# Batch 0's head: q by head halves, narrow weight slices and a reordered chain

## The chip, the cores and the metric

One NeuronCore of a Trainium2 chip runs the whole kernel. The metric is the device time of one execution in microseconds (us); lower is better. "Span" is the time from the first to the last instruction that the profile shows; the device time is 1.7 to 2.0 us longer in all executions of the kernel before that are listed with their spans. Two times within 2% of each other are called the same.

## The reference, cut to what matters

```python
def _attn_ref(q, k, v, g_norm):                    # q, k, v: 8 batches x 8 heads x 576 x 64
    kv = np.einsum('bhsd,bhse->bhde', k, v)        # K^T V, 64 x 64 per head
    out = np.einsum('bhsd,bhde->bhse', q, kv)      # scores
    rms = np.sqrt(np.mean(out * out, axis=-1, keepdims=True) + 1e-06)
    return out / rms * g_norm

def reference(...):
    x = attn_out.transpose(0, 2, 1, 3).reshape(4608, 512)
    h = x @ w_in                                   # w_in: 512 x 2048
    g = np.where(h > 0.0, h, np.exp(np.minimum(h, 0.0)) - 1.0)
    return g @ w_out                               # w_out: 2048 x 512
```

## The kernel before

Eight batches of 512 rows and a ninth group made of the leftover rows go through attention, a first layer and a second layer. From some 20 us on, TensorE works nearly without pause. Only batch 0's beginning is special: its x is made transposed, in four column parts c (two heads each), because nothing else can keep TensorE busy yet. The helpers of that head:

```python
    def kv_first(c):                       # K^T V of the heads of part c, cast to bf16 on VectorE
        u, l = c // 2, c % 2
        kv_single(0, kv_ps, u, (l,))
        ls = slice(l * 64, l * 64 + 64)
        nc.vector.tensor_copy(out=kv0[ls, u], in_=kv_ps[ls, :, u * 64 : u * 64 + 64])

    def se_first(c):                       # scores of part c: needs q of pairs u and 2 + u
        u, l = c // 2, c % 2
        ls = slice(l * 64, l * 64 + 64)
        for s in range(2):
            nc.tensor.matmul(se0[c][s * 64 : s * 64 + 64, :], lhsT=kv0[ls, u, s, :],
                             rhs=qT0[ls, 2 * s + u, :], start=True, stop=True)

    def square_first(c):  nc.scalar.activation(sq0[c], se0[c], AF.Square)
    def mean_first(c):    nc.tensor.matmul(mean0[c], lhsT=means, rhs=sq0[c], start=True, stop=True)
    def log_first(c):     nc.scalar.activation(r0[c], mean0[c], AF.Ln, bias=eps_col)
    def exp_first(c):     nc.scalar.activation(r0[c], r0[c], AF.Exp, scale=-0.5)
    def scale_first(c):   nc.vector.scalar_tensor_tensor(out=x0[:, c, :], in0=se0[c], scalar=g_col,
                                                         in1=r0[c], op0=ALU.mult, op1=ALU.mult)
    def first(fs, cs):                     # products of w_in's column blocks f with x's parts c
        for c in cs:
            for f in fs:
                nc.tensor.matmul(products[f], lhsT=w_in_sb[:, c, f * P : f * P + P], rhs=x0[:, c, :],
                                 start=(c == 0), stop=(c == KC - 1))
    def idle(ps, n):                       # dummy products on zeros, to keep TensorE's clock up
        for _ in range(n):
            nc.tensor.matmul(ps, lhsT=zeros[:, 0:P], rhs=zeros, start=True, stop=True)
```

(Formatting of the one-line helpers is condensed here.) The loads and the order of the head before the change:

```python
    fetch_q(0)                             # two 512 KB loads on SyncE's queue: even heads, then odd heads
    ...                                    # k and v in four parts each on GpSimd's queue, cast to bf16 on the way
    edges = (0, 512, 768, 1280, 1664, 2048)
    for lo, hi in zip(edges, edges[1:]):
        load_w_in(slice(lo, hi))           # 512 rows x (hi - lo) columns, also on GpSimd's queue, cast to bf16
    ...
    idle(idle_ps, 9)
    ...                                    # cast and transpose q of pairs 0, 1; idle(idle_ps, 4); then q of pair 2
    kv_first(0); idle(idle_ps, 1); se_first(0); square_first(0)
    ...                                    # transpose q of pair 3
    kv_first(1); mean_first(0); log_first(0); se_first(1); square_first(1); exp_first(0)
    ...                                    # g_col, one tiny product
    kv_first(2); idle(idle_ps, 2); se_first(2); square_first(2)
    mean_first(1); log_first(1); exp_first(1)
    idle(idle_ps, 1); kv_first(3); scale_first(0); idle(idle_ps, 1)
    mean_first(2); log_first(2); se_first(3); square_first(3); exp_first(2)
    idle(bank(0), 2); scale_first(1); scale_first(2)
    first((0, 1, 2, 3), (0,))
    mean_first(3); log_first(3); exp_first(3); scale_first(3)
    first((0, 1, 2, 3), (1, 2)); first((4,), (0, 1, 2)); first((0, 1, 2, 3), (3,))
    first((5,), (0, 1, 2)); first((4, 5), (3,))
    ...
    for i in range(3, 8):
        mm1(0, i, ...)()                   # from here on: the regular stream of TensorE
```

Later, batch 1's attention is woven into batch 0's second layer (`mm2`); its second K^T V (`at["kvu1"]()`) came after step j == 1 of one of those loops.

## Time and profile before

| | kernel before |
|---|---|
| time, median of 3 | 284.08 us (284.08 to 284.27) |
| the profiled execution | 284.47 us, span 282.7 us |
| first v part landed | 7.81 us |
| first scores | 8.96 us |
| first product with w_in | 14.76 us |
| last part of x scaled | 17.43 to 18.18 us |
| regular stream starts | 20.27 us |

In the timeline, each line gives start, microseconds taken, engine, source line, operation, what it writes and reads, the shape, and how many instructions were joined; brackets at the end give how long the engine had been idle and who ended that. PEld is the load of weights into TensorE. "L465" is the first layer's product in the kernel before. The lines that the prediction quotes stand there; three more of the kernel before matter, from the timeline of the head (K^T V of part 0; the products with the last scaled part; the start of the stream):

```profile
8.11 0.47 PE L174 MATMUL kv_ps<-v_pk,k_pk 64*64 64x64 bf16 x18
...
18.33 0.59 PE L674 MATMUL h_ps<-xT,w_in_sb 128*128 128x512 bf16 x2
...
20.27 0.59 PE L465 MATMUL h_ps<-xT,w_in_sb 128*128 128x512 bf16 x2
```

The first is the start of K^T V, which needs v (landed at 7.81): it began 0.3 us after that.

### The profile page before, as it was taken

How to read it: one execution, taken by the hardware profiler on the slowest of the kernel's cores; microseconds unless marked ns; L12 is line 12 of the kernel's file. 1: busy time of each engine (PE TensorE's matmuls, PEld its weight loads, DVE VectorE, ACT ScalarE, POOL GpSimd, SP SyncE). 2: the span in 40 equal slices, each digit the busy share in tenths (PEclk: the TensorE clock that was granted, in tenths of full speed). 3: DMA queues.
4: the chain of work that ended last, by engine and by line, in shares of the span. 5: the costliest groups of instructions: out<-in, count | busy, mean ns of one | idle time of the engine just before them, and what ended most of it. 6: DMA issues, size and time to landing. Idle time of an engine off the chain costs nothing.

```text
span 282.7 us, 5187 instructions
## 1 busy us (share of the span) xinstructions
PE 277.2 (98%) x2146; PEld 129.7 (46%) x2146; DVE 159.3 (56%) x231; ACT 154.5 (55%) x222; POOL 54.7 (19%) x96
## 2 busy tenths in 40 slices
PE   7999999999999999999999999999999999999994
PEld 3444454445444444444444444444444444444443
DVE  2359443878388646944694468445854585444400
ACT  2779546667487438533863377237923792333311
POOL 7834422261421331005200421012000000000000
PEclk9999999999999999999999999999999999999999
DMA  7999999797993696358935794455233122010122
GB/s 194 203 204 202 208 200 185 220 152 129 187 190 62 154 166 148 74 148 124 196 75 145 93 216 84 116 115 150 55 97 73 78 53 95 0 77 0 74 74 77
DMA packets 56523, 35.99 MB, mean 127 GB/s; under 512 B 32820, under 2 KB 54068, under 8 KB 56500
## 3 DMA queue, kind: packets, MB, share of 16 engines
q0 software_dynamic: 20752, 17.30, 39.9%
q1 hardware_dynamic: 35348, 17.83, 23.7%
q10 hardware_dynamic: 400, 0.52, 0.6%
q8 instruction: 17, 0.28, 0.4%
q14 instruction: 6, 0.05, 0.0%
HBM read 36.70 MB, written 9.44 MB: 163 GB/s over the span
## 4 chain that ended last, share of the span: by engine, by line
PE 95%; DMA 2%; DVE 1%; SPq 0%; issue 0%; ACT 0%
PE h_ps L465 41%; PE o_ps L512 39%; PE o_ps L917 5%; DMA st_q<-in_q_dram 2%; PE at L174 2%; PE bank L674 1%; PE at L465 1%; PE at L201 1%; PE h_ps L674 1%; PE bank L596 1%; PE bank L644 1%; PE se_ps L201 1%; PE kv_ps L174 0%; PE at L185 0%; PE se_ps L413 0%; PE bank L656 0%
## 5 line engine op out<-in xcount | busy, mean ns | idle before, releaser
L465 PE MATMUL h_ps<-xT,w_in_sb 128*128 128x512 bf16 x536 | 125.7, 379 | 0.0
L512 PE MATMUL o_ps<-w_out_sb,gT 128*128 128x512 bf16 x512 | 120.5, 379 | 0.0
L477 ACT ACTIVATE elu_e<-h_ps 128x1024 bf16<-128x1024 f32 (+1 forms) x71 | 70.0, 995 | 79.9 <-PE h_ps L465 78.3
L465 PEld LDWEIGHTS <-w_in_sb 128*128 128x128 bf16 x552 | 52.5, 98 | 63.2 <-DVE xT L333 1.7
L512 PEld LDWEIGHTS <-gT 128*128 128x128 bf16 x512 | 49.4, 98 | 58.4
L488 DVE TENSOR_SCALAR elu_e<-elu_e 128x1024 bf16<-128x1024 bf16 (+1 forms) x75 | 32.3, 431 | 72.9 <-ACT elu_e L477 72.9
L496 DVE TENSOR_TENSOR gT<-elu_e,h_ps 128x1024 bf16<-128x1024 bf16 (+1 forms) x51 | 60.1, 1179 | 5.7 <-DVE elu_e L488 0.5
L525 ACT COPY o_sb<-o_ps 128x512 f32<-128x512 f32 x32 | 18.6, 586 | 15.6 <-PE o_ps L512 15.6
L218 DVE TENSOR_REDUCE ss<-sq 128x16 f32<-128x1024 bf16 x16 | 19.4, 1219 | 10.8 <-ACT sq L213 10.1
L483 ACT ACTIVATE elu_h<-h_ps 128x1024 bf16<-128x1024 f32 (+1 forms) x20 | 19.5, 990 | 0.0
L150 POOL COPY q_bf<-q_pk 128x512 bf16<-128x512 bf16 x24 | 14.6, 638 | 21.6 <-DMA q_pk<-in_q_dram 21.6
L496 DVE TENSOR_TENSOR gT<-elu_e,elu_h 128x1024 bf16<-128x1024 bf16 x20 | 13.8, 692 | 2.9 <-ACT elu_h L483 1.5
L917 PE MATMUL o_ps<-w_out_sb,gT 128*128 128x512 bf16 (+1 forms) x80 | 14.1, 337 | 0.0
L125 POOL COPY gate<-qT 1x1 bf16<-1x1 bf16 x6 | 1.1, 182 | 63.7 <-DMA qT<-q_bf 63.7
L104 POOL DMA_DIRECT2D q_pk<-in_q_dram x14 | 10.6, 762 | 2.8 <-issue 1.1
L229 DVE TENSOR_TENSOR xs<-at,ss 128x512 bf16<-128x512 f32 x16 | 10.3, 682 | 1.2 <-ACT ss L225 1.2
L917 PEld LDWEIGHTS <-gT 128*128 128x128 bf16 x80 | 7.7, 98 | 6.4 <-DVE gT L496 0.4
L213 ACT ACTIVATE sq<-at 128x1024 bf16<-128x1024 f32 x9 | 9.4, 1043 | 1.6 <-PE at L201 1.0
L118 POOL DMA_DIRECT2D k_pk<-in_k_dram x12 | 8.3, 691 | 4.5 <-DMA w_in_sb<-in_moe_w_in_dram 2.9
L596 PE MATMUL bank<-zeros 128*128 128x512 bf16 x20 | 7.8, 515 | 1.2 <-DVE zeros L573 1.2
L118 POOL DMA_DIRECT2D v_pk<-in_v_dram x12 | 8.2, 684 | 3.7 <-DMA w_out_sb<-in_moe_w_out_dram 1.8
L925 ACT COPY o_last<-o_ps 128x512 f32<-128x512 f32 (+1 forms) x5 | 2.5, 501 | 10.8 <-PE o_ps L917 10.8
(79 smaller groups left out, 139.4 us busy)
## 6 DMA issues: line engine op xcount, KB each, us to landing
out_dram<-o_sb SPq DMA_DIRECT2D x16, 512.0 KB, 3.0
q_pk<-in_q_dram POOLq DMA_DIRECT2D x14, 256.0 KB, 4.8
k_pk<-in_k_dram POOLq DMA_DIRECT2D x6, 576.0 KB, 8.3
v_pk<-in_v_dram POOLq DMA_DIRECT2D x6, 576.0 KB, 10.8
st_q<-in_q_dram SPq DMA_DIRECT2D x2, 512.0 KB, 5.1
w_in_sb<-in_moe_w_in_dram POOLq DMA_DIRECT2D x2, 512.0 KB, 8.8
w_out_sb<-in_moe_w_out_dram POOLq DMA_DIRECT2D x2, 512.0 KB, 15.2
w_out_sb<-in_moe_w_out_dram POOLq DMA_DIRECT2D x4, 256.0 KB, 11.8
```

What stands on the lines that cost most here:

```text
L118: nc.gpsimd.dma_start(out=raw[name, b].rearrange("p h j d -> p h (j d)")[:, hs], in_=in_[:, hs])
L150: eng.tensor_copy(out=out_, in_=in_)
L218: nc.vector.reduce_sum(out=ss, in_=sq.rearrange("p c (h e) -> p (c h) e", h=H), axis=AX.X)
L465: nc.tensor.matmul(h_ps[a][:, cs], lhsT=w_in_sb[:, c, f * P : f * P + P], rhs=x(c, cs), start=(c == 0), stop=(c == KC - 1),)
L477: nc.scalar.activation(e[:, lo:hi, :], ps, AF.Exp)
L483: nc.scalar.activation(h[:, lo:hi, :], ps, AF.Relu)
L488: nc.vector.tensor_scalar(out=e[:, lo:hi, :], in0=e[:, lo:hi, :], scalar1=1.0, scalar2=1.0, op0=ALU.min, op1=ALU.subtract,)
L496: nc.vector.tensor_tensor(out=gT[T][:, 2 * i + lo : 2 * i + hi, :], in0=e[:, lo:hi, :], in1=h, op=ALU.add if relu else ALU.max,)
L512: nc.tensor.matmul(o_ps[T, j], lhsT=gT[T][:, f, j * P : j * P + P], rhs=w_out_sb[:, f, :], start=(f == 0), stop=(f == FC - 1),)
L525: nc.scalar.copy(o_sb[T][:, j % 2, :], o_ps.pop((T, j)))
L596: nc.tensor.matmul(ps, lhsT=zeros[:, 0:P], rhs=zeros, start=True, stop=True)
L917: nc.tensor.matmul(ps, lhsT=gT[B][:, f, j * P : j * P + P], rhs=w_out_sb[:, f, cols], start=(f == 0), stop=(f == FC - 1),)
```

## The change

The intent is to start the regular stream earlier by closing the waits of the head: feed the first scores from the first half of q, keep ScalarE's chain (square, logarithm, exponential) dense, get the first weights sooner in narrower slices, and do the products slice by slice. The core of the diff, with cuts marked:

```diff
-    fetch_q(0)
-    q_raw0 = raw.pop(("q", 0))
+    q_raw0 = stage_tile("q")[:, 0:2048].rearrange("p (u x) -> p u x", u=2)
+    for u in range(2):
+        nc.sync.dma_start(
+            out=q_raw0[:, u].rearrange("p (h x) -> p h x", h=4),
+            in_=q[0, 4 * u : 4 * u + 4, 0:G, :].rearrange("h (p j) d -> p h (j d)", j=J),
+        )
...
-    edges = (0, 512, 768, 1280, 1664, 2048)
+    edges = (0, 256, 512, 768, 1024, 1280, 1664, 2048)
...
-    cast_first(1, A)
+    cast_first(2, A)
...            # pairs 0 and 2 are cast and turned first, then 1 and 3
+    g_ps = bank(2)                                   # g_col's product, moved up from behind exp_first(0)
+    nc.tensor.matmul(g_ps[:, 0:1], lhsT=..., rhs=one, start=True, stop=True)
+    nc.vector.tensor_copy(out=g_col, in_=g_ps[:, 0:1])
     kv_first(0)
-    idle(idle_ps, 1)
+    turn_last(7, 1)                                  # transpose of q, now behind K^T V; copy on VectorE
...
     kv_first(2)
-    idle(idle_ps, 2)
+    mean0[1] = bank(0)
+    mean_first(1)
+    log_first(1)
+    idle_ps = bank(3)
     se0[2] = bank(1)
     se_first(2)
     square_first(2)
-    mean0[1] = bank(0)
-    mean_first(1)
-    log_first(1)
     exp_first(1)
+    scale_first(0)
     idle(idle_ps, 1)
     kv_first(3)
-    scale_first(0)
-    idle(idle_ps, 1)
...
-    idle(bank(0), 2)
...
-    first((0, 1, 2, 3), (0,))
+    first((0, 1), (0, 1))
     mean0[3] = bank(2)
     mean_first(3)
...
-    first((0, 1, 2, 3), (1, 2))
+    first((2, 3), (0, 1))
+    first((0, 1, 2, 3), (2,))
     first((4,), (0, 1, 2))
-    first((0, 1, 2, 3), (3,))
-    first((5,), (0, 1, 2))
-    first((4, 5), (3,))
+    first((0, 1, 2, 3, 4), (3,))
+    first((5,), range(KC))
...
+    at["inv0"]()
+    at["mulu0"]()
     for j in range(J):
         mm2(0, j, 8, 10)
-        if j == 1:
+        if j == 2:
             at["kvu1"]()
-            at["inv0"]()
-            at["mulu0"]()
...            # mm1 gets by_c: batch 1's first block runs part of x by part of x
```

## The prediction

> **What bounds the kernel now.** I read the page first, then its chain of work that ended last, then the engines' busy time by stretch, and then the timeline of the first 47 us, for only that part is touched.
>
> ```profile
> span 282.7 us, 5187 instructions
> PE 277.2 (98%) x2146; PEld 129.7 (46%) x2146; DVE 159.3 (56%) x231; ACT 154.5 (55%) x222; POOL 54.7 (19%) x96
> PEclk9999999999999999999999999999999999999999
> ...
> PE 95%; DMA 2%; DVE 1%; SPq 0%; issue 0%; ACT 0%
> ```
>
> TensorE (PE) is busy for 277.2 of 282.7 us and is 95% of the chain. In the view of busy time by stretch (start:end, length, busy us and instruction count, clock, DMA share, GB/s):
>
> ```profile
> 5.49:20.27 14.78, 14.57 (x137) 1.00 1.26 206
> 20.27:46.69 26.42, 26.42 (x257) 1.00 1.28 204
> 46.69:282.70 236.01, 232.17 (x1745) 1.00 0.54 112
> ```
>
> Two things are to be seen. From 20.27 us on, where the regular first-layer products of batch 0 begin, PE has no wait of note: whatever starts that stream d us earlier ends the kernel d us earlier, unless a wait opens behind it. And through 46.69 us the DMA engines are saturated, near 205 GB/s of written bytes, so data can be reordered there, not hurried. Before 20.27 PE is called busy, but part of it is dummy products on zeros. The timeline of that head (start, us taken, what, idle time before and its releaser):
>
> ```profile
> 6.32 1.40 PE L596 MATMUL bank<-zeros 128*128 128x512 bf16 x4
> ...
> 7.30 0.43 DVE L150 CAST q_two<-st_q 128x512 bf16<-128x512 f32 x1
> ...
> 8.96 0.40 PE L644 MATMUL bank<-qT,kv 64*64 64x512 bf16 x2
> ...
> 11.56 0.63 ACT L662 ACTIVATE r<-r 128x512 f32<-128x512 f32 x1
> ...
> 12.56 0.60 ACT L653 ACTIVATE sq<-bank 128x512 bf16<-128x512 f32 x1 [0.37 <-PE bank L644]
> ...
> 13.06 0.68 ACT L659 ACTIVATE r<-bank,eps_col 128x512 f32<-128x512 f32 x1
> ...
> 13.77 0.63 ACT L662 ACTIVATE r<-r 128x512 f32<-128x512 f32 x1
> 13.83 1.41 DVE L665 SCALAR_TENSOR_TENSOR xT<-bank,g_col,r 128x512 bf16<-128x512 f32 x2
> ...
> 14.76 0.55 PEld L674 LDWEIGHTS <-w_in_sb 128*128 128x128 bf16 x4 [0.39 <-DMA w_in_sb<-in_moe_w_in_dram]
> ...
> 16.05 0.69 ACT L659 ACTIVATE r<-bank,eps_col 128x512 f32<-128x512 f32 x1
> ...
> 16.77 0.63 ACT L662 ACTIVATE r<-r 128x512 f32<-128x512 f32 x1
> ...
> 17.43 0.75 DVE L665 SCALAR_TENSOR_TENSOR xT<-bank,g_col,r 128x512 bf16<-128x512 f32 x1 [0.67 <-ACT r L662]
> ```
>
> The head makes x of batch 0 in four column parts c: K^T V, scores (L644), square, mean on PE, logarithm (L659), exponential (L662), scaling (L665). Then 24 products (L674) precede 20.27. They begin at 14.76, released by the first 512 columns of w_in. From 14.76 to 20.27 are 5.51 us; 24 products and one mean are 25 matmuls at 0.216 us (from L465: 24 in 5.34 us, so (5.34 - 0.38) / 23) = 5.40 us. So only 0.11 us of that stretch is waiting. The bounds are thus the landing of the weights (14.76) and, nearly as tight, the last scaled part: it ends at 18.18 and its first product starts at 18.33.
>
> **What the Trainium skill says.** (1) "TensorE: Matmul & The Clock Gate", section "Part 1: The HAM clock gate": PE runs at half clock until about 3.4 us of sustained work and falls back after an idle window. The trace agrees: the nine dummy products from 1.22 us take 4.02 us, (4.02 - 0.38) / 8 = 0.455 us apart at most, against 0.216 later; weight loads shrink from 0.15 to 0.10 us at 7.12. (The clock row says 1.00 throughout, so matmul spacing is the better witness.) (2) "ScalarE: Activation LUTs", section "What ACT_TABLE_LOAD costs": an activation of 512 columns costs 186 + 427 = 613 ns, 93 ns more with a pointer bias, and neighbours overlap by about 93 ns. The trace agrees: 0.63 us exponential, 0.69 us logarithm with bias, successive starts 0.48 to 0.58 us. (3) "DMA: Bandwidth & Descriptors", section "Issuing engines are not separate DMA queues": all queues share 16 engines. The trace agrees: q from SyncE and k, v from GpSimd split a constant rate. (4) Same page, "Specifications": 512 B is the least size at line rate. A slice of 256 bf16 columns writes 512 B per row; the stretches 24 to 26 and 40 to 42 us, mostly such packets, moved 195 GB/s, 27 to 29 us with larger ones 206. So a small loss is there.
>
> **The change part by part.**
> 1. Q by head halves. Before, the first scores needed both halves of q (landed 4.98 and 7.28 us), and a transpose after the second. Now heads 0 to 3 come first and serve parts 0 and 1 alone. But the first K^T V needs v, issued at 1.92 and landing 5.9 us later, 7.8. Before it started at 8.11, behind four transposes. Now those follow it, and only the g product (0.3 us, moved up from 10.87) precedes it: start 7.9, first scores at 8.75 instead of 8.96: 0.2 us. VectorE takes over one qT copy (0.42 us), on time.
> 2. Tightened chain. Means come before the next scores, and six of 20 dummy products go. Chaining with the trace's durations: ACT starts square 0 at 9.23, log 0 10.31, square 1 10.89, exp 0 11.37, log 1 11.94, square 2 12.52, exp 1 13.0, log 2 13.57, square 3 14.14, exp 2 14.62. Before, exp 2 started at 15.36, because after exp 0 (11.56) ACT idled until 12.56. The gain has grown to 0.74 us. The last mean starts at 14.93, behind four products: log 3 at 15.36, exp 3 at 16.08, scaling 16.74 to 17.49, against 18.18 before: 0.69 us.
> 3. w_in in narrow slices. k and v end at 12.17 (5.66 + 6.5). 256 columns are 0.26 MB, at 195 GB/s 1.34 us: slices land at 13.5, 14.85, 16.2, where 512 columns landed at 14.7. The third may suffer: before, 256 columns issued at 8.12 took 8.9 us and landed at 17.05, 2.3 us after the preceding 512. The page counts 17 instruction fetches of 16 KB on another queue; one near 15 us on the slowest DMA engine would explain the extra microsecond. I take 17.1.
> 4. Products slice by slice: f 0, 1 of part 0 at 13.73; part 1 waits for its scaling, 14.5; mean 14.93; f 2, 3 from 15.15 to 16.0; part 2 (scaling ends 16.05) 16.1 to 16.96; f 4 waits for the third slice, 17.1 to 17.75; part 3 of five blocks to 18.83; f 5 four products to 19.69. The regular stream starts at 19.7 instead of 20.27: 0.58 us. With the third slice on time it is 19.55, 0.72 us.
> 5. Cost behind it: 1.05 MB in 512 B instead of 1 KB pieces, 5.37 instead of 5.07 us: all later loads land 0.3 us later. The second v part of batch 1, issued at 25.92, lands 11.9 us later, 37.8; its use was at 38.85. 1.0 us of slack less 0.6 and 0.3 leaves almost nothing; two products moved ahead of it give 0.43 back. Moving the first part's normalisation ahead of that copy on ACT holds the next transposes' scaling on time; I allow 0.1 us of stall at the second scores, where logarithm, exponential and copy now queue on ACT. Running batch 1's first block by column part saves nothing: x's second half was ready at 46.42, before the block started at 46.69.
> Six dummies at 0.216 us are 1.3 us of PE work, but they filled waits and count nothing by themselves.
> Sum: 0.58 to 0.72, less 0 to 0.1: about 0.6 us, 0.2%. 284.08 - 0.6 = 283.5.
>
> **The rivals.** (a) Clock: fewer dummies might let PE fall to half clock. For it: the skill's rule. Against it: before, 8.1 to 11.5 us held about 2.2 us of issuing work in 3.4 us (65%) and stayed fast; my schedule has about 66% and 68% in the two windows before the products. If it happened, 25 products at double spacing cost 2 to 5 us: 286 to 288. (b) DMA takes over: the fetch or the narrow packets delay slice two or three by one more microsecond, or v of batch 1 comes late; the gain shrinks to 0 to 0.2: 283.9 to 284.1. For it: saturated queue, slices arriving at the very moment of use. (c) All waits close: 25 matmuls from 13.73 end at 19.13, gain 1.1: 282.9. Against it: scalings of parts 1 and 3 come later than PE would be ready. (d) Elu of the first blocks: their PSUM banks are released in another order. Before, exp of the first block waited 1.56 us for PE; it shifts with the products, so I see no new wait.
>
> **Range and chances.** Between (b) and (c) lie 282.9 and 284.1; repeats agree to 0.2 us. I give 282.9 to 284.0. 2% is 5.7 us: faster would need more than the whole idle part of the head, 1%; slower only by a lasting half clock, 1%; within 98%.
>
> **What would show it.** The first scores near 8.75 us; no ACT idle between exp 0 and square 2; the first w_in product near 13.7; the wait before f 4 (DMA) or its absence; the last scaling ending near 17.5; the regular stream at 19.6 to 19.7; no PE wait at the second K^T V of batch 1 near 38.7. It would be wrong if weight loads in the head return to 0.15 us, if a product waits for w_in by more than 0.5 us, or if the stream starts earlier and the end does not.

## The result, and the profile after

| | before | after |
|---|---|---|
| median of 4 runs | 284.08 us | 283.81 us |
| range | 283.98 to 284.27 | 283.61 to 284.56 |
| profiled execution | 284.47 us, span 282.7 | 283.69 us, span 281.9 |

The ratio is 0.9995, with a 95% interval of 0.9975 to 1.0014: the same. All ratios here are the mean time of one kernel's fast runs over that of the other's fast runs of the same rounds, so not quite the ratio of the quoted medians.

The page of the kernel after: span, busy time, the clock row and the chain that ended last.

```profile
span 281.9 us, 5175 instructions
...
PE 275.6 (98%) x2140; PEld 129.1 (46%) x2140; DVE 160.5 (57%) x232; ACT 153.8 (55%) x221; POOL 56.1 (20%) x98
...
PEclk9999999999999999999999999999999999999999
...
PE 94%; DMA 2%; ACT 1%; DVE 0%; SPq 0%; issue 0%
```

Busy time by stretch after, cut at the start of the regular stream and at batch 1's first block (columns as in the prediction, with the other engines between):

```profile
5.22:19.47 14.25, 12.77 (x132) 6.00 (x130) 6.54 (x14) 8.81 (x15) 9.88 (x14) 1.00 1.32 199
19.47:45.88 26.41, 26.41 (x258) 12.93 (x257) 16.51 (x25) 17.84 (x29) 8.86 (x13) 1.00 1.28 204
45.88:281.90 236.02, 232.42 (x1745) 108.73 (x1743) 136.28 (x187) 125.26 (x176) 33.29 (x60) 1.00 0.55 113
```

The second and third stretch last 26.41 and 236.02 us, where before they lasted 26.42 and 236.01: behind the start of the stream nothing changed. All of the trace's gain, 20.27 - 19.47 = 0.80 us, was made in the head. The timeline of that head after:

```profile
7.67 0.47 PE L174 MATMUL kv_ps<-v_pk,k_pk 64*64 64x64 bf16 x18
...
8.52 0.40 PE L652 MATMUL bank<-qT,kv 64*64 64x512 bf16 x2
...
11.09 0.63 ACT L670 ACTIVATE r<-r 128x512 f32<-128x512 f32 x1
...
11.67 0.69 ACT L667 ACTIVATE r<-bank,eps_col 128x512 f32<-128x512 f32 x1
...
12.26 0.59 ACT L661 ACTIVATE sq<-bank 128x512 bf16<-128x512 f32 x1
...
13.53 0.33 PEld L682 LDWEIGHTS <-w_in_sb 128*128 128x128 bf16 x3 [0.23 <-DMA w_in_sb<-in_moe_w_in_dram]
...
15.77 0.63 ACT L670 ACTIVATE r<-r 128x512 f32<-128x512 f32 x1
...
16.43 0.75 DVE L673 SCALAR_TENSOR_TENSOR xT<-bank,g_col,r 128x512 bf16<-128x512 f32 x1 [0.64 <-ACT r L670]
...
16.87 2.27 PEld L682 LDWEIGHTS <-w_in_sb 128*128 128x128 bf16 x12 [0.50 <-DMA w_in_sb<-in_moe_w_in_dram]
...
19.47 1.24 PE L467 MATMUL h_ps<-xT,w_in_sb 128*128 128x512 bf16 x5
```

K^T V of part 0 starts 0.09 us after v landed (7.58) instead of 0.30. The logarithm of part 1 now follows the first exponential at once (11.67), and square 2 follows it (12.26) with no idle time in its brackets; before, there were 0.37 us there and the logarithm came after. The products begin at 13.54. The brackets of their weight load name the first 256 columns of w_in, but those had landed at 13.27: the product follows 0.33 us behind the scores of part 3 (13.20), as the dummies there did before (13.93 and 14.26), so it is TensorE's own order that holds it now, and no load. The third slice is waited for at 16.87: [0.50 <-DMA] is the weight load's wait; TensorE's own excess wait there, read from the starts of its products, is 0.17 us. The last scaling starts at 16.43 instead of 17.43.

So the trace gained 0.8 us but the medians only 0.27 us. Two things had to be found out: which parts of the change make the gain, and why the usual execution gains less than the profiled one.

### The profile page after: what moved, and what is told of

Its sections match the earlier page's. It is cut to its first block, busy times and chain, and to the rows that moved or that the text cites. A ratio compares the mean times of both kernels' runs of the same rounds, so it can differ in the third digit from the quotient of the medians.

```text
span 281.9 us, 5175 instructions
## 1 busy us (share of the span) xinstructions
PE 275.6 (98%) x2140; PEld 129.1 (46%) x2140; DVE 160.5 (57%) x232; ACT 153.8 (55%) x221; POOL 56.1 (20%) x98
## 4 chain that ended last, share of the span: by engine, by line
PE 94%; DMA 2%; ACT 1%; DVE 0%; SPq 0%; issue 0%
PE h_ps L467 42%; PE o_ps L514 39%; PE o_ps L922 5%; DMA g_row<-in_g_norm_dram 2%; PE at L174 2%; PE bank L682 1%; PE at L467 1%; PE at L201 1%; PE h_ps L682 1%; PE se_ps L201 1%; ACT r L667 0%; ACT r L670 0%; PE at L185 0%; ACT sq L661 0%; SPq L555 0%; PE se_ps L413 0%
## 5 line engine op out<-in xcount | busy, mean ns | idle before, releaser
L490 DVE TENSOR_SCALAR elu_e<-elu_e 128x1024 bf16<-128x1024 bf16 (+1 forms) x75 | 32.9, 438 | 73.0 <-ACT elu_e L479 73.0
L218 DVE TENSOR_REDUCE ss<-sq 128x16 f32<-128x1024 bf16 x16 | 19.4, 1218 | 11.1 <-ACT sq L213 10.4
L174 PEld LDWEIGHTS <-k_pk 64*64 64x64 bf16 x576 | 6.4, 107 | 4.1 <-issue 3.9
```

Source lines behind the costliest of these rows:

```text
L174: nc.tensor.matmul(kv_ps[l * 64 : l * 64 + 64, s, u * 64 : u * 64 + 64], lhsT=bf["k", T][rows, j, 2 * u + l, :], rhs=bf["v", T][rows, j, 2 ...
L218: nc.vector.reduce_sum(out=ss, in_=sq.rearrange("p c (h e) -> p (c h) e", h=H), axis=AX.X)
L490: nc.vector.tensor_scalar(out=e[:, lo:hi, :], in0=e[:, lo:hi, :], scalar1=1.0, scalar2=1.0, op0=ALU.min, op1=ALU.subtract,)
```

## The experiments

Each is an edit of the kernel after. All results were correct. The kernel before was run on the same chip with each set; its medians were 284.14 us (first four experiments), 284.26 us (next four) and 284.16 us (last two), with spans of 282.2 to 282.7. What the traces showed, in one table (readings of the traces in us; "stream" is the start of the regular stream, "rest" is span minus stream, "v" the landing of the first v part, "fetch" the start of the one instruction fetch in the head, a packet of 16 KB):

| kernel | v | first product | fetch | stream | span | rest |
|---|---|---|---|---|---|---|
| before | 7.81 | 14.76 | 15.01 | 20.27 | 282.7 | 262.4 |
| after | 7.58 | 13.54 | 14.27 | 19.47 | 281.9 | 262.4 |
| again | 7.95 | 13.85 | 14.78 | 19.60 | 281.8 | 262.2 |
| wide_slices | 7.97 | 14.92 | 14.87 | 20.34 | 282.5 | 262.2 |
| old_chain | 8.03 | 14.43 | 15.02 | 20.06 | 282.2 | 262.2 |
| kv_early | 8.05 | 13.95 | 14.83 | 19.82 | 282.1 | 262.3 |
| wide_filled | 7.86 | 15.24 | 14.39 | 20.65 | 282.8 | 262.2 |
| no_dummies | 7.90 | 14.62 | 15.54 | 21.12 | 283.3 | 262.2 |
| filled | 8.06 | 14.13 | 14.76 | 19.88 | 282.6 | 262.7 |
| parity_q | 7.56 | 13.89 | 14.37 | 19.64 | 281.8 | 262.2 |
| q_late | 7.27 | 14.46 | 15.48 | 20.30 | 282.5 | 262.2 |
| no_by_c | 7.66 | 13.55 | 14.30 | 19.55 | 281.9 | 262.4 |

The last column is the first result: over twelve traces, whose stream starts 1.65 us apart, the rest stays within 262.2 to 262.4 us but for one (262.7). Whatever moves the stream moves the end.

### again: the kernel after, unchanged

> The changed kernel unaltered, for a second trace and more timings, since its four runs ranged over 0.95 us where the kernel before ranged over 0.3. Theory: the trace's gain (regular first-layer stream starts at 19.47 us instead of 20.27) is a property of the kernel, so this trace starts the stream at 19.4 to 19.8 us and the median is 0.4 to 0.8 us below the kernel before. Rival: part of the 0.8 us was luck with one lagging DMA engine (q's first half landed at 4.4 us instead of 5.0), so the stream starts at 19.9 or later and the median gains under 0.3 us.

No edit. Measured: 283.91 us median of 6 (283.75 to 285.21), ratio 0.9999 (0.9986 to 1.0013). Spans were 281.8, 282.2, 282.8, 282.1, 282.2 and 282.0, against 282.2 to 282.4 for the kernel before in the same set. So the kernel after is usually 0.2 to 0.4 us shorter but scatters more, and one long run (285.21) pulls its mean back to the other's. In this trace v landed 0.37 us later than in the first one (7.95) and the stream started at 19.60. So the stream came where the theory put it (19.4 to 19.8), but the median gained only 0.23 us, as the rival had it (under 0.3). The scatter is not noise of the clock or the counter alone: the loads land differently from one execution to the next. In part it stays unexplained: the run of 285.21 us has a span of only 282.8, so 2.4 us lie outside it.

### wide_slices: the old slices of w_in, everything else new

```diff
-    edges = (0, 256, 512, 768, 1024, 1280, 1664, 2048)
+    edges = (0, 512, 768, 1280, 1664, 2048)
```

> Only w_in's first columns go back to the old cuts (512, 256, 512 columns); chain, order of products and the rest stay changed. Theory (weights bound the start of the products): the first product moves from 13.5 to 14.3 to 14.8 us, the mean of the last part, which sits behind four products, moves to 15.6, and the regular stream starts at 20.1 to 20.4 us: nearly all of the gain is gone, the time is that of the kernel before within 0.2 us. Rival (the chain of squares, logarithms and exponentials sets the end): the stream still starts at 19.5 to 19.7.

Measured: 285.25 us median of 6, ratio 1.0051 (1.0023 to 1.0080). The executions fall in two groups: three at 284.14 to 284.60 us with spans of 282.4 to 282.5 and a mean clock of 0.999 to 1.0, and three at 285.89 to 287.03 us with spans of 284.0 to 284.2 and a mean clock of 0.994. The trace is of the first group:

```profile
14.92 1.04 PE L682 MATMUL h_ps<-xT,w_in_sb 128*128 128x512 bf16 x4 [0.98 <-DMA w_in_sb<-in_moe_w_in_dram]
```

TensorE stands still until the first 512 columns land, and the stream starts at 20.34, no earlier than in the trace before: without narrow slices, the tightened chain is worth nothing. The second group was not expected, and no execution of it was traced. A mean clock of 0.994 over 284 us is a loss of 0.006 x 284 = 1.7 us at full rate, about the 1.6 us by which these spans are longer; at half rate that is one stretch of 3.4 us. (Means of 0.997 to 0.999 are no such fall in the head: in the four traces that have one, filled, parity_q, q_late and no_by_c, the clock record halves only in the last 1.1 to 1.7 us of the span.) Whether TensorE's idle time brings the clock down was tested by wide_filled and no_dummies.

### old_chain: scores 2 ahead of mean 1, three dummies put back

```diff
     kv_first(2)
-    mean0[1] = bank(0)
-    mean_first(1)
-    log_first(1)
     idle_ps = bank(3)
+    idle(idle_ps, 2)
     se0[2] = bank(1)
     se_first(2)
     square_first(2)
+    mean0[1] = bank(0)
+    mean_first(1)
+    log_first(1)
     exp_first(1)
-    scale_first(0)
     idle(idle_ps, 1)
     kv_first(3)
+    scale_first(0)
+    idle(idle_ps, 1)
```

> Only the head's chain goes back: scores of part 2 and their square ahead of the mean of part 1, and the dummy products between are back; narrow slices, halves of q and slice-by-slice products stay. Theory: exp 2 starts 0.4 to 0.6 us later (about 14.9), the last scaling ends near 17.8, five plus four products follow it, and the regular stream starts at 19.8 to 20.1 us: 0.3 to 0.6 us slower than the changed kernel. Rival (only the slices matter, the chain had slack): stream at 19.5 to 19.6.

Measured: 284.31 us median (283.89 to 285.22), ratio 1.0009 (0.9997 to 1.0022). The first product now waits for x, not for weights:

```profile
14.43 1.25 PE L682 MATMUL h_ps<-xT,w_in_sb 128*128 128x512 bf16 x4 [0.30 <-DVE xT L673]
```

The stream starts at 20.06, 0.46 us behind the one of "again", in which v landed 0.08 us earlier. So the order of the chain is worth about 0.4 us on top of the narrow slices. The three dummies are a rival for little of it: scores 2 start no later behind VectorE's cast of K^T V (0.15 us after its end) than in "again" (0.19), and what comes later is the logarithm of part 1, at 12.85 instead of 11.98. The second scaling, behind which TensorE waits no more, starts at 14.29, 0.10 us after its exponential ended; at most that much could be the dummies'. With the old order the chain is the bound, with the wide slices it was the weights. That is the prediction's reading of before, where both bounds lay close together. Two of the six executions had spans of 283.0 and 283.4; no trace shows why.

### kv_early: batch 1's second K^T V back at j == 1

```diff
-    at["inv0"]()
-    at["mulu0"]()
     for j in range(J):
         mm2(0, j, 8, 10)
-        if j == 2:
+        if j == 1:
             at["kvu1"]()
+            at["inv0"]()
+            at["mulu0"]()
```

> Only batch 1's second K^T V goes back one step (after two products of the step instead of three pairs) with its normalisation behind it, as before; the faster head stays. Theory: PE reaches it at 38.05 us, its v lands at 38.2, so PE waits 0.1 to 0.2 us there and the first transposes of x wait another 0.2 to 0.4 us for the scaling: end 0.2 to 0.5 us later than the changed kernel. Rival: this part of the change is worth nothing, PE shows no excess there and the time is the same within 0.1 us.

Measured: 284.00 us median (283.82 to 285.08), ratio 1.0003 (0.9990 to 1.0015). This expectation failed. TensorE around that point:

```profile
38.44 0.48 PE L174 MATMUL at<-v_pk,k_pk 64*64 64x64 bf16 x36
...
41.07 0.61 PE L413 MATMUL se_ps<-ident,xs 128*128 128x128 bf16 x8
```

From the last product to K^T V there is a gap of 0.351 us (0.310 in the kernel after), and before the transposes at 41.07 there are 0.038 us too many. Together that is less than 0.1 us. K^T V ran at 38.44, about when it runs in the kernel after (38.48), because the stream of this execution began 0.35 us later. So the move was not needed in this execution. With an earlier stream it would be tighter: in the trace of the kernel after, K^T V two products earlier would come at 38.05, but its v landed at 38.21, a wait of some 0.2 us (an estimate from these figures; no run shows it).

### wide_filled: old slices, and five dummies in front of the first product

```diff
-    edges = (0, 256, 512, 768, 1024, 1280, 1664, 2048)
+    edges = (0, 512, 768, 1280, 1664, 2048)
...
     exp_first(2)
+    idle(bank(0), 5)
     scale_first(1)
```

> The wide cuts of the second experiment, plus five dummy products on PE in the wait ahead of the first w_in product (1.1 us of issue in a gap of 1.2 us). Of wide_slices' six executions three had a span of 284.0 to 284.2 us at a mean clock of 0.994, three 282.4 to 282.5 at 1.0. Theory (the idle PE lets the clock fall to one half for one window of about 3.4 us, which costs 0.006 of the span's clock and 1.6 us): with the gap filled no execution shows 0.994, all spans lie within 282.3 to 282.8 and the median is 284.1 to 284.5. Rival (the slow executions come from the DMA queue or from the chip, not from PE's idleness): still some at 0.994 or above 283.5 us of span.

Measured: 284.75 us median of 5 (284.26 to 284.89), ratio 1.0010 (0.9997 to 1.0023), spans 282.5 to 282.8, mean clock at least 0.999 in every execution. Not one fell to 0.994. The stream still starts late (20.65), so the dummies do nothing for the data, and the median missed the expected 284.1 to 284.5. Three of six against none of five is not many, and the two sets ran on different chips. The mean clock of the second group and the next run make it very likely that idle time of TensorE brought its clock down; by these counts alone it is not shown.

### no_dummies: the kernel after without its dummies behind the first nine

```diff
-    idle(idle_ps, 4)
     cast_first(1, V)
...
     scale_first(0)
-    idle(idle_ps, 1)
     kv_first(3)
```

> The changed kernel without the five dummy products that it keeps after the first nine. No dummy is on the critical path of the changed kernel's trace, so if PE's clock did not matter the time would be the same within 0.1 us (rival). Theory: more idle PE in the head, so several executions fall to half clock for a window: some at a clock of 0.994 with spans of 283 to 284.5, median 284.3 or more.

Measured: 285.65 us median (285.06 to 286.33), ratio 1.0048 (1.0033 to 1.0063); the mean clock was 0.982 to 0.988 in all six executions, where only some at 0.994 were expected. Busy time by stretch in its trace, cut where the clock record changes (the last three columns are clock, DMA share and GB/s):

```profile
6.64:10.05 3.41, 2.44 (x49) 1.76 (x49) 1.94 (x7) 1.22 (x2) 2.58 (x4) 1.00 1.20 198
10.05:13.46 3.41, 3.08 (x42) 1.77 (x42) 1.39 (x4) 2.94 (x6) 3.37 (x5) 0.50 1.35 198
13.46:16.88 3.42, 3.12 (x8) 1.02 (x9) 1.70 (x3) 2.23 (x5) 1.73 (x3) 0.50 1.45 197
16.88:21.12 4.24, 4.24 (x21) 1.86 (x19) 1.00 (x2) 2.63 (x4) 1.91 (x3) 1.00 1.36 201
```

The clock is 0.50 from 10.05 to 16.88, two stretches of 3.41 us, although TensorE is "busy" for 2.44 of the 3.41 us before. Busy time is not a measure of work here: a lone product of 512 columns counts 0.38 us, while in a stream one starts every 0.216 us. So the five dummies that this edit removes do nothing for the data flow, stand on no path that sets the end, and are still worth 1.5 us (stream at 21.12 against 19.60 in "again", where v and the first slice landed within 0.05 us of here). The kernel after with 14 dummies kept a mean clock of at least 0.998 in all executions of "again"; it had taken away six of 20.

### filled: five more dummies in TensorE's waits

```diff
+    idle(idle_ps, 1)
     kv_first(0)
...
+    idle(idle_ps, 1)
     se0[1] = bank(7)
...
+    idle(idle_ps, 1)
     kv_first(2)
+    idle(idle_ps, 1)
     mean0[1] = bank(0)
...
     kv_first(3)
+    idle(idle_ps, 1)
     mean0[2] = bank(2)
```

> The changed kernel plus five more dummy products, each in a wait of PE that its trace shows (before the first K^T V, before the scores of part 1, before K^T V 2, before means 1 and 2). Theory (the tail of the changed kernel's times, up to 285.2, is PE's clock): the spread shrinks to under 0.4 us, median 283.7 to 283.9, no execution over 284.2; this would beat both. Rival (the tail is late data: a w_in slice held up on one DMA engine): the tail stays, some execution over 284.4.

Measured: 284.10 us median of 5 (283.64 to 284.34), ratio 0.9990 (0.9978 to 1.0002), spans 281.9 to 282.6. Its slowest run is 284.34, where "again" had one of 285.21; but its median is no better, so the expectation (median 283.7 to 283.9, none over 284.2) failed. In its trace v landed at 8.06 and the stream started at 19.88. Not all five dummies fitted into waits: the one ahead of mean 1 (11.62) put that mean at 11.85, and the logarithm of part 1 came 0.75 us after exponential 0 instead of 0.58. This held the chain by 0.17 us, so the run adds dummies and takes away part of the gain at once. I can't tell from five runs whether the shorter tail comes from the dummies.

### parity_q: q by even and odd heads, as before

```diff
-    for u in range(2):
-        nc.sync.dma_start(out=q_raw0[:, u]..., in_=q[0, 4 * u : 4 * u + 4, 0:G, :]...)
+    fetch_q(0)
...
-    cast_first(2, A)
+    cast_first(1, A)
     qt_ps = turned(3)
-    turn_first(qt_ps, (0, 2))
+    turn_first(qt_ps, (0, 1))
...
-    cast_first(1, V)
+    cast_first(2, V)
...
-    turn_last(7, 1)
+    turn_last(7, 2)
```

> Only q goes back to halves by odd and even heads, so the first scores need both halves and one more copy. Prediction's step 1 (worth 0.2 us): first scores at 8.9 to 9.1 us instead of 8.5 to 8.8, the chain behind shifts by 0.2 to 0.4 and the regular stream starts 0.2 to 0.4 us later, at 19.8 to 20.0. Rival (arrivals of k and v set the chain anyway): stream within 0.1 us of the changed kernel's.

Measured: 283.98 us median of 5 (283.45 to 284.55), ratio 0.9989 (0.9977 to 1.0001). Here v landed at 7.56, as in the trace after (7.58), so the two can be laid side by side. The scores of part 0 and the first square:

```profile
8.45 0.84 PE L646 MATMUL bank<-qT,kv 64*64 64x512 bf16 x2
...
9.32 0.60 ACT L655 ACTIVATE sq<-bank 128x512 bf16<-128x512 f32 x1 [1.70 <-PE bank L646]
```

The two products take 0.84 us instead of 0.40, since the second waits for the copy of the late half of q; the square starts at 9.32 instead of 8.97. Of these 0.35 us only 0.17 reach the stream (19.64 against 19.47), for in the kernel after the third slice is waited for (0.17 us), and here the later chain covers that wait. So the stream lies between the theory (19.8 to 20.0) and the rival (within 0.1 us). The times don't tell the two kernels apart, and this is one pair of traces. So the head halves are worth at most 0.2 us, as the prediction had put it.

### q_late: half of q behind the first k and v, on GpSimd's queue

```diff
+    fetch_half(0, nc.sync)
...
         fetch_packed_kv("v", 0, slice(c, c + 1))
+        if c == 0:
+            fetch_half(1, nc.gpsimd)
...            # the second half is cast and turned behind scores 0; exponential 0 and scaling 0 move up;
               # 19 dummies instead of 14 (by count of the edit; the expectation says seven more)
```

> The changed kernel with the thought of q's halves carried on: heads 4 to 7, not used before the scores of part 2, are loaded behind the first k and v instead of ahead of them, their cast and transposes follow the first scores, and seven more dummies lie in PE's waits. In the traces so far v of part 0 landed at 7.56 to 8.06 us and the regular stream started 11.8 to 11.9 us later. Theory (that landing sets the head): it lands near 6.3, the first scores are at 7.1 to 7.4, part 0's chain runs ahead, and ACT, no longer the bound from its first operation on, ends exp 3 0.2 to 0.5 us earlier; the stream starts at 19.0 to 19.4, the span is 281.3 to 281.8, the median 283.1 to 283.6. Rival (w_in's slices and ACT's own work set the end): first scores move by a microsecond, the stream by less than 0.1.

The idea was that v, which starts everything, should not queue with a half of q that is needed later. Measured: 284.42 us median (284.30 to 285.56), ratio 1.0020 (1.0006 to 1.0034). The theory failed. v landed at 7.27, only 0.3 us earlier and far from the 6.3 hoped for, and everything behind it came later: the last part of k and v at 12.87 instead of 11.94, the slices of w_in at 14.21, 15.60 and 17.66 instead of 13.27, 14.67 and 16.82. The stream follows the third slice: from 17.66 twelve products at 0.216 us lead to 20.30, as they lead from 16.82 to 19.47 in the kernel after. One stretch of each trace shows a part of the loss, first of q_late, then of the kernel after (last column GB/s):

```profile
7.50:9.00 1.50, 1.33 (x21) 0.47 (x15) 0.69 (x3) 0.40 (x1) 0.91 (x2) 1.00 1.13 177
```

```profile
7.50:9.00 1.50, 1.45 (x29) 0.99 (x30) 0.87 (x3) 0.18 (x2) 1.50 (x3) 1.00 1.21 202
```

Care is needed here: the view counts bytes written. Loads of k, v and w_in read f32 and write bf16, while q is cast only later, so stretches with different loads don't compare. From 3.0 to 4.5 us, q_late wrote 292 GB/s and the kernel after 382, but the bytes read, with the casting loads counted twice, were 383 and 382 GB/s. The stretch shown has nearly only k and v in the kernel after, and in q_late also the end of its half of q, which can only raise its figure; still it is lower. Over 1.5 to 13.5 us the kernel after moved 2.66 MB and q_late 2.54 MB (sums over eight stretches of 1.5 us, GB/s times time). 0.12 MB is 0.6 us at 200 GB/s, two thirds of the 0.9 us by which its slices were late; the rest is not accounted for. The edit changes both the queue of that half and its place among the loads, and which of the two lowers the rate was not separated.

### no_by_c: batch 1's first block in the old order

```diff
-        mm1(1, i, ..., by_c=i == 0)()
+        mm1(1, i, ...)()
```

> Only batch 1's first block goes back from column part by column part to block by block. Prediction: worth nothing, since x's second half was ready 0.3 us before the block began; PE shows no excess gap there, and the span from the start of the regular stream to the end is the same within 0.05 us. Rival: a wait of 0.1 to 0.4 us appears before the block's third product.

Measured: 284.22 us median of 4 (283.87 to 284.81), ratio 1.0009 (0.9995 to 1.0024). The stream started at 19.55 and 262.4 us remained, as in the kernel after; no wait stands ahead of that block in either trace. The part does nothing, as predicted.

## Why the prediction was right, and where its steps were off

The prediction said 283.5 us and "within 2%"; 283.81 lies in its range. By itself that says little: the range ended 0.08 us below the kernel before, and the four runs after spread over 0.95 us. What counts is whether its steps came as worked out.

**The bound.** Right. The rest behind the stream stayed at 262.4 us in both traces and at 262.2 to 262.7 in all twelve.

**The chain.** Right to the tenth, but for a constant. Worked out for squares 0 to 3: 9.23, 10.89, 12.52, 14.14; measured 8.97, 10.62, 12.26, 13.89. Exponential 2: 14.62 against 14.37; last scaling 16.74 against 16.43; stream 19.7 against 19.47. Every step came 0.23 to 0.31 us early, that is, by the difference in the first step: v landed at 7.58 instead of the assumed 7.8. The chained durations were right; the time of the first arrival was copied from one trace. One sentence of the working needs a qualification: that q, k and v "split a constant rate" holds for bytes read (375 to 409 GB/s in the stretches of 1.5 us from 3 to 12 us of the kernel before, casting loads counted twice), not for the bytes written that the view shows (381 at 4 to 5 us, 205 at 8 to 9).

**The slices.** Worked out 13.5, 14.85 and 17.1 (with the instruction fetch), measured 13.27, 14.67 and 16.82: again early by a constant, 0.2 to 0.3 us, and the wait for the third slice came where it had been put. The guess that an instruction fetch delays one slice is supported by all twelve traces: each has one fetch packet in the head, starting between 14.27 and 15.54 and taking 0.89 to 0.97 us. The sixteenth and last piece of each load lands a little behind the eighth, and this lag grows by 0.43 to 0.98 us at the slice then in flight. In the kernel after, the lag is 0.38 us for the second slice and 1.22 us for the third. In no_dummies, with fewer instructions and a later fetch (15.54), it hits the fourth slice and spares the third. Which DMA engine moved the fetch is not in the records, so the cause is well supported but not proved.

**The size of the sum.** Here the step was off. I worked the gain out as 0.6 us against the trace before, and took it off the median, 284.08. But the profiled execution of before was not a median one: it took 284.47 us and its span was 282.7, where the other executions listed had mostly 282.2 to 282.4. In its head one piece of every load trailed: the first half of q landed at 4.98, while 15 of its 16 pieces were there at 4.47; v at 7.81, 15 pieces at 7.32; the first slice at 14.72, 15 pieces at 14.21. The trace after had no lone straggler of that size before its third slice (v 7.58, 15 pieces at 7.56). So the trace gained 0.80 us, of which the prediction's own steps explain 0.57 and the earlier start 0.23, and the usual execution gained about 0.2 to 0.4 us of span: the median span of its ten executions is 282.05, against mostly 282.2 to 282.4. A difference that is taken from one trace belongs to that trace's own time: 284.47 - 0.8 is 283.7, and that is what the profiled execution after took (283.69).

**The parts.** Narrow slices and the new chain together make the gain (stream at 19.47 to 19.88). The new chain without narrow slices gains nothing (wide_slices, 20.34 against 20.27), the narrow slices without the new chain 0.2 us (old_chain, 20.06, although its v landed 0.2 us later than before). The head halves gave 0.17 us in a pair of traces with equal arrival of v, predicted 0.2. by_c gave nothing, as predicted. The 0.1 us allowed for a stall at batch 1's scores was not seen.

**The rivals.** (a) The clock: it did not fall in the kernel after, as expected, but it was nearer than I had reckoned (the 1% was for a half clock that lasts). That dropped dummies "count nothing by themselves" was right for the six and would have been wrong for the next five. Leaving the slices wide dropped half of the executions to a mean clock of 0.994, and five dummies fewer dropped all. A penalty of 2 to 5 us had been named; measured were 1.5 us for two half-rate stretches (no_dummies, at the stream) and about 1.6 us of span for the executions of wide_slices at 0.994. (b) The DMA as the new bound: in part true. The kernel after begins its chain the moment v lands, so it passes any lateness of v on (v 7.58 to 8.06 and stream 19.47 to 19.88, over the five traces of after, again, no_by_c, kv_early and filled, in the same order). The kernel before waited for 512 columns of w_in instead, which hid part of this. That the lateness goes through the chain can be read off: in again and parity_q, where no slice was waited for, the stream started 10.32 us after square 0 in both; in after, no_by_c and kv_early it was 10.43 to 10.56, and the wait for the third slice there was 0.10 to 0.22. That the old wait hid part of v's lateness would explain why the kernel before repeats more evenly, but this is argued from these traces and not shown by a run of its own. (c) All waits closed: did not happen; the third slice and the two scalings still hold TensorE for 0.13 to 0.22 us each. (d) No new wait at the ELU: right, the rest did not change.

Still open: why some executions of the changed kernels take up to 3.2 us more than their span (before: 1.7 to 2.0), and what lets one piece of a load trail in some executions and not in others.

## What to carry to other kernels

When two waits lie close together at the head of a pipeline, remove both or neither, and test each alone to see it: here each half of the change was worth nothing or little by itself. Count dummy work that keeps TensorE's clock up as part of the schedule, and before you remove it, see whether the clock record or the mean clock of repeated executions drops. Take a gain that you worked out on a trace off that trace's own time, not off the median, and check whether the profiled execution was a usual one.

## What the Trainium skill lacked or had wrong

- "TensorE: Matmul & The Clock Gate", section "HAM oscillation — how this bites in real kernels", gives the rule that no idle gap may exceed some 3.4 us. Shorter ones were enough here: in no_dummies the longest gap between starts of products ahead of the fall was 1.34 us, and the clock was 0.50 for 6.83 us; in wide_slices three of six executions had a mean clock of 0.994 with a longest gap of 1.4 us in the profiled one, which was not one of the three. The page's next section does say that frequent short idle times can make the clock swing, but how much work makes a window count as busy is not stated; these runs bracket it only by kernels, not by a number. That the window is 3.41 us long and runs freely, as the page's "Part 1: The HAM clock gate" has it, agrees: in no_dummies the record changes 3.41 us after it begins and again 6.83 us later, and in the twelve traces it turned to full at different times between 4.00 and 7.10 us.
- "DMA: Bandwidth & Descriptors", section "Issuing engines are not separate DMA queues", says that issuing from several engines saves only the time to issue. Where half of q was moved from SyncE's queue to GpSimd's and behind the first k and v (q_late), the slices of w_in landed 0.9 us later, and the rate from 7.5 to 9.0 us was 177 instead of 202 GB/s. Since the place changed with the queue, this does not refute the page; it shows that such a move is not free.
- The same page, section "Latency and other measured facts", says that DMA engines 7 and 15 are usually slower than the others, but not by how much: here a load of 16 pieces ended 0.3 to 1.2 us behind its middle piece (the first v part, twelve traces; which engine it was is not in the records). "Runtime: NRT & Kernel Launch", section "Instruction fetch mechanics", calls the cost of fetching the next 16 KB of instructions mostly hidden; that one such fetch, of 0.89 to 0.97 us, goes with a further 0.43 to 0.98 us for the load in flight is on no page.
